# First head pair of an attention kernel: the second head's codes of k behind the second exponential, codes of q's second half one step later

## The chip, the cores and the metric

The kernel runs on one core of a Trainium2 chip. The metric is device time in microseconds (us), from launch to the end of the program. A profiled execution also has a span, from its first to its last instruction.

The core has five engines, each with its own queue that it works off in order, and they meet at semaphores: TensorE (PE in the profile; its weight loads are PEld), VectorE (DVE), ScalarE (ACT), GpSimd (POOL) and SyncE (SP), which here issues the DMAs.

## The reference

Attention with hashed masks over 4 batches of 8 heads (768 positions, 64 wide), followed by a mixture of 8 experts with one expert for each token. Cut to what matters:

```python
scale = 1.0 / np.sqrt(D)
q_bits = (np.einsum('bhsd,dk->bhsk', q, proj) > 0)          # 6 bits; k_bits alike
mask = q_bucket[:, :, :, None] == k_bucket[:, :, None, :]   # all 6 bits equal
scores = np.where(mask, scale * q @ k.T, -1e9)
attn = softmax(scores)
x = (attn @ v)                                              # 3072 tokens of 512
e = argmax(x @ w_gate, axis=1)
out = gate * (relu(x @ w1[e]) @ w2[e])
```

## The kernel before

**Tiling.** The 32 heads are worked in 16 pairs. A pair has six blocks of 128 queries for each of two heads, so 12 steps; there are 192 steps in all, and the list `steps` gives for each step i its pair, its group of three blocks, its block and its head. In pair 0 the first six steps are blocks 0, 1, 2 of head 0 and then blocks 0, 1, 2 of head 1; steps 6 to 11 take blocks 3, 4, 5, head 0 and head 1 in turn. After the attention the tokens, scattered by expert into a buffer in DRAM, are gathered and pass through the two products of each expert.

**A step.** `scores` (L220) makes 128 rows of scores with four products: q and k are each split into a high part (q1, k1) and a low part, and q2 and k2 carry the codes, 12 more rows that push a pair of unequal buckets far below all others. VectorE takes the maximum m (L228 to L230), `expo` (L233) lets ScalarE make p with its sums, `transposes` (L260) turns p on TensorE and ScalarE copies it out (L268), and `av` (L278) multiplies by v. The loop over i runs ahead: in round i it writes the scores of step i+2, then the exponential of step i+1, then the transposes of step i. Scores have two banks (`s`), transposes two (`t`), codes of q and some other small work one (`misc`).

**Operands.** For pairs from 1 on, q and k are split by GpSimd (`q_operands`, `k_operands`: L161 to L163 and L167 to L169), their codes are made by `pair_codes` (L143: a product into `misc` or `t` at L148, compared with 0 at L150, scaled at L151) and placed by DMA (`code_rows`, L176). The table `PREPARE` says in which round: for pair 1, both heads' q in round 2, codes and the first head's k in round 3.

Pair 0 has functions of its own. `first_k` (L181) makes one head's k1 and k2 and a product for its codes in both banks `t`; it returns a function that compares them (L200, VectorE, two instructions) and scales them (L201, ScalarE, two). `first_q` (L205) does the same for half of a head's q: a product into `misc` (L210), casts (L212, L213 on VectorE for the second half; L215, L216 on ScalarE for the first), the low part on GpSimd (L217), and a returned function that compares (L218, VectorE). The second halves are not needed before step 6 (head 0) and step 7 (head 1).

**What sets the order.** PE, DVE, ACT and SP carry out their work in the order in which the program writes it. GpSimd's work on q, k and codes is held in the order of writing too, each instruction by a dependence on the one before it:

```python
def in_turn(ins):
    ins = ins.ins
    if pinned:
        tc.add_manual_dep(ins, pinned.pop().name, mybir.DependencyInfo(mybir.DependencyClass.NoSync, mybir.DependencyReason.DATA),
                          reason="order of GpSimd's work on q, k and codes")
```

The pool of q's and k's raw tiles of pair 0 is closed (`start.close()`) in round 3.

Of the kernel before, what the change touches and what calls it, by code (L numbers as in the profile page):

```python
# [52 lines left out]
def bf(ap):  # L53
    return ap.bitcast(F32)
# [3 lines left out]
def lsh_attention_moe_kernel(ctx, tc, qkd, q2d, k2d, v, pjbd, wg, w1, w2, ident_in, tri_in, cols_in, eoff_in, ids_in, out):  # L58
# [64 lines left out]
# [5 lines that stand above are left out]
        if not in_turn_over:  # L128
            pinned.append(ins)
# [51 lines left out]
    def first_k(hh, low):  # L181
        kr = operands[0][0][hh][1]
        k1, k2 = operands[0][0][hh][4:6]
        cpss = []
        for x in range(2):
            cps = ps_t.tile([P, 512], F32, name="t")
            r0 = D + 32 * x
            PE.matmul(out=cps[r0:r0 + 32, 0:384], lhsT=pj, rhs=kr[:, 384 * x:384 * x + 384], start=True, stop=True)
            cpss.append(cps[r0:r0 + NCODE, 0:384])
        if hh:  # L190
            A.copy(out=k1, in_=kr)
        else:
            V.tensor_copy(out=k1, in_=kr)
        low.tensor_tensor(out=k2[0:D], in0=kr[0:D], in1=bf(k1[0:D]), op=ALU.subtract)

        def put_codes():
            for x in range(2):
                cs = slice(384 * x, 384 * x + 384)
                r0 = D + 32 * x
                V.tensor_scalar(out=k2[D:KM, cs], in0=cpss[x], scalar1=0.0, scalar2=cols[r0:r0 + NCODE, 2:3], op0=ALU.is_gt, op1=ALU.subtract)  # L200
                A.activation(k2[D:KM, cs], bf(k2[D:KM, cs]), AF.Copy, bias=0.0, scale=BIG)  # L201

        return put_codes

    def first_q(hh, c0):  # L205
        qr = operands[0][0][hh][0]
        q1, q2 = operands[0][0][hh][2:4]
        cps = ps_m.tile([P, 512], F32, name="misc")
        cs = slice(c0, c0 + 384)
        PE.matmul(out=cps[0:32, 0:384], lhsT=pj, rhs=qr[:, cs], start=True, stop=True)  # L210
        if c0:
            V.tensor_copy(out=q1[:, cs], in_=qr[:, cs])  # L212
            V.tensor_copy(out=q2[0:D, cs], in_=qr[0:D, cs])  # L213
        else:
            A.copy(out=q1[:, cs], in_=qr[:, cs])  # L215
            A.copy(out=q2[0:D, cs], in_=qr[0:D, cs])  # L216
        in_turn(G.tensor_tensor(out=q1[D:P, cs], in0=qr[D:P, cs], in1=bf(q1[D:P, cs]), op=ALU.subtract))  # L217
        return lambda: V.tensor_scalar(out=q2[D:KM, cs], in0=cps[0:NCODE, 0:384], scalar1=0.0, scalar2=cols[0:NCODE, 0:1], op0=ALU.is_gt, op1=ALU.subtract)  # L218
# [14 lines left out]
    def expo(s, m, sums, idx, moves):  # L233
        if moves:
            p = pdp.tile([P, S], F32, name="pd")
            to, of = p.rearrange("p (a c i) -> p c a i", a=4, i=SQ), s[:, 0:S].rearrange("p (c a i) -> p c a i", a=4, i=SQ)
        else:
            p = pp.tile([P, S], F32, name="p")
            to, of = p, s[:, 0:S]
        A.activation(to, of, AF.Exp, bias=m[:, 2:3], scale=m[:, 1:2], accum_out=sums[:, idx:idx + 1])  # L240
        return p

    def move(p, pt, hh):
        way = moved[next(writes) % 2]
        q = pdp.tile([P, 4, 6, SQ], F32, name="pq")
        to = way.rearrange("(a j) s k -> s j a k", a=4)

        def out():
            for x in range(4):
                SY.dma_start(out=to[x], in_=p[SQ * x:SQ * x + SQ].rearrange("j (a k) -> j a k", a=4))  # L250

        def back():
            SY.dma_start(out=q, in_=way.rearrange("p s (c i) -> p s c i", i=SQ))

        def turn():
            V.transpose(out=pt()[:, hh].rearrange("p c (s j) -> p c s j", j=SQ), in_=q.rearrange("p s c i -> p c s i"))

        return out, back, turn
# [305 lines left out]
    def sums_of(pr, g):  # L564
        if (pr, g) not in grp:
            grp[(pr, g)] = smp.tile([P, 6], F32, name="sums", bufs=4)
        return grp[(pr, g)]

    def run_expo(i):
        pr, g, jj, hh = steps[i]  # L570
        moves = i % 6 in MOVES.get((pr, g), ())
        p = expo(*soft.pop(i), sums_of(pr, g), 2 * jj + hh, moves)
        if moves:
            out, back, turn = move(p, partial(probs_t, pr, g, jj), hh)
            later.extend([(i, out), (i + 2, back)])
            turns.append((i + 5, turn))
        else:
            probs[i] = p

    def run_scores(i):  # L580
        pr, g, jj, hh = steps[i]
        soft[i] = scores(pr, 3 * g + jj, hh)
# [158 lines left out]
    first_codes = [first_k(0, V), first_q(0, 0)]  # L741
# [3 lines left out]
    run_scores(1)  # L745
    first_codes = [first_k(1, G), first_q(1, 0)]
    run_expo(0)
    for f in first_codes:
        f()
    SY.dma_start(out=h0[0][:, 384:S], in_=q2d[0][:, 384:S])  # L750
    prev, due, extra = None, [], {}
    for i, (pr, g, jj, hh) in enumerate(steps):
# [27 lines left out]
            prefill(i // 6 - 1)  # L780
        if i + 2 < len(steps):
            run_scores(i + 2)
        if 1 <= i < 3:
            first_q(i - 1, 384)()
        if i == 3:
            start.close()
        if i + 1 < len(steps):
            run_expo(i + 1)
        while late:
            late.pop(0)()  # L790
        sums = sums_of(pr, g)
# [439 lines left out]
```

## Time and profile before

| | us |
|---|---|
| median of 3 runs | 748.88 |
| the runs | 747.42, 748.88, 756.24 |
| profiled execution | 746.31 |
| its span | 744.5 |
| TensorE busy in the span | 717.5 (96%) |
| VectorE busy | 527.4 (71%) |
| ScalarE busy | 457.9 (62%) |
| GpSimd busy | 384.5 (52%) |

The profiled execution took 1.8 us more than its span. The mean granted TensorE clock was 0.993 of full speed. A row of the timeline reads: start in us, duration in us, engine, line, operation, output, input, shapes, count, and in brackets how long the engine had stood idle and what released it. Where several instructions of a kind follow each other they are merged into one row, with the time from the first start to the last end.

### The profile page before, as it was taken

How to read it: one execution, taken by the hardware profiler on the slowest of the kernel's cores; microseconds unless marked ns; L12 is line 12 of the kernel's file. 1: busy time of each engine (PE TensorE's matmuls, PEld its weight loads, DVE VectorE, ACT ScalarE, POOL GpSimd, SP SyncE). 2: the span in 40 equal slices, each digit the busy share in tenths (PEclk: the TensorE clock that was granted, in tenths of full speed). 3: DMA queues.
4: the chain of work that ended last, by engine and by line, in shares of the span. 5: the costliest groups of instructions: out<-in, count | busy, mean ns of one | idle time of the engine just before them, and what ended most of it. 6: DMA issues, size and time to landing. Idle time of an engine off the chain costs nothing.

```text
span 744.5 us, 16345 instructions
## 1 busy us (share of the span) xinstructions
PE 717.5 (96%) x5919; PEld 632.3 (85%) x5919; DVE 527.4 (71%) x1158; ACT 457.9 (62%) x941; POOL 384.5 (52%) x366
## 2 busy tenths in 40 slices
PE   6999999999999999999989998999999999999996
PEld 3788888877888778888777887999999999999994
DVE  6667776887887888887899776674747465566741
ACT  5888887777888678888677865343434334344430
POOL 2877337098436187634485242007474738364381
PEclk8999999999999999999999999999999999999999
DMA  5166666666666567666664531746556565657531
GB/s 185 50 192 165 195 182 189 187 194 189 178 183 190 170 203 196 166 181 188 176 180 131 160 90 59 209 105 177 146 175 152 189 165 161 188 154 226 165 91 43
DMA packets 85259, 121.45 MB, mean 163 GB/s; under 512 B 10758, under 2 KB 57382, under 8 KB 85168
## 3 DMA queue, kind: packets, MB, share of 16 engines
q1 hardware_dynamic: 80176, 107.61, 51.3%
q0 software_dynamic: 4992, 12.69, 4.9%
q8 instruction: 49, 0.80, 0.5%
q14 instruction: 42, 0.34, 0.1%
HBM read 79.04 MB, written 39.24 MB: 159 GB/s over the span
## 4 chain that ended last, share of the span: by engine, by line
PE 45%; issue 22%; POOL 13%; DVE 11%; DMA 5%; SPq 2%; ACT 1%; POOLq 0%; DVEq 0%
PE o L283 14%; POOL y L1007 10%; PE t L265 9%; PE s L225 9%; PE s L226 7%; DVE m L228 4%; DMA y<-yo,tags 2%; POOL yo L1005 1%; PE misc L315 1%; PE t L148 1%; DMA qk<-qkd 1%; DMA xr<-xs 1%; DVE m L230 1%; SPq L176 1%; ACT p L240 1%
## 5 line engine op out<-in xcount | busy, mean ns | idle before, releaser
L228 DVE TENSOR_REDUCE m<-s 128x1 f32<-128x768 f32 x192 | 182.6, 951 | 48.4 <-PE s L226 41.4
L240 ACT ACTIVATE p<-s,m 128x768 f32<-128x768 f32 x144 | 143.3, 995 | 42.0 <-DVE m L230 27.8
L225 PE MATMUL s<-k,q 128*128 128x512 f32 (+1 forms) x384 | 149.2, 389 | 7.8 <-ACT p L240 5.2
L283 PE MATMUL o<-pt,vt 128*64 128x128 f32 x2304 | 146.7, 277 | 0.2
L268 ACT COPY pt<-t 128x384 f32<-128x384 f32 x288 | 123.9, 482 | 34.3 <-PE t L265 31.2
L283 PEld LDWEIGHTS o<-pt,vt 128*64 128x64 f32 x2304 | 123.8, 137 | 14.8 <-issue 7.4
L226 PE MATMUL s<-k,q 76*128 76x512 f32 (+1 forms) x384 | 123.9, 343 | 0.2 <-DVE q L218 0.2
L265 PE MATMUL t<-ident,p 128*128 128x128 f32 x864 | 120.0, 274 | 3.2 <-DVE cr L150 3.1
L1007 POOL DMA_INDIRECT y<-yo,tags x89 | 103.3, 1161 | 25.2 <-issue 22.9
L225 PEld LDWEIGHTS s<-k,q 128*128 128x128 f32 x384 | 73.2, 191 | 44.4 <-issue 15.0
L265 PEld LDWEIGHTS t<-ident,p 128*128 128x128 f32 x864 | 99.0, 141 | 6.7 <-DVE cr L150 4.0
L965 ACT ACTIVATE hh<-hps 128x352 fp32r<-128x352 f32 (+3 forms) x56 | 28.0, 500 | 99.3 <-PE hps L979 88.6
L682 DVE TENSOR_TENSOR wlo<-wraw,whi 128x1024 fp32r<-128x1024 f32 x60 | 73.0, 1219 | 17.0 <-ACT whi L677 16.0
L226 PEld LDWEIGHTS s<-k,q 76*128 76x128 f32 x384 | 73.7, 192 | 9.3 <-ACT k L201 0.5
L998 PE MATMUL hps<-hh,wlo 128*128 128x436 f32 (+6 forms) x224 | 76.2, 340 | 0.0
L998 PE MATMUL hps<-hh,whi 128*128 128x448 f32 (+10 forms) x224 | 76.2, 340 | 0.0
L998 PE MATMUL hps<-hl,whi 128*128 128x436 f32 (+6 forms) x224 | 76.2, 340 | 0.0
L979 PE MATMUL hps<-xh,whi 128*128 128x352 f32 (+3 forms) x224 | 75.0, 335 | 0.0
L979 PE MATMUL hps<-xh,wlo 128*128 128x428 f32 (+6 forms) x224 | 74.8, 334 | 0.0
L979 PE MATMUL hps<-xl,whi 128*128 128x428 f32 (+6 forms) x224 | 74.8, 334 | 0.0
L1005 POOL TENSOR_TENSOR yo<-yt,tags 128x512 f32<-128x512 f32 (+3 forms) x25 | 23.4, 959 | 88.1 <-DVE yt L1000 88.0
L966 DVE SCALAR_TENSOR_TENSOR hl<-hps,hh 128x352 fp32r<-128x352 f32 (+3 forms) x56 | 31.7, 566 | 48.6 <-ACT hh L965 45.0
(225 smaller groups left out, 1202.1 us busy)
## 6 DMA issues: line engine op xcount, KB each, us to landing
wraw<-w SPq DMA_DIRECT2D x64, 512.0 KB
moved<-pd SPq DMA_DIRECT2D x192, 96.0 KB
pq<-moved SPq DMA_DIRECT2D x48, 384.0 KB
qk<-qkd SPq DMA_DIRECT2D x30, 384.0 KB
xs<-zrow SPq DMA_DIRECT2D x8, 910.0 KB
vt<-v SPq DMA_DIRECT2D x16, 384.0 KB
xr<-xs SPq DMA_DIRECT2D x12, 178.8 KB
xr<-xs SPq DMA_DIRECT2D x8, 227.5 KB
```

What stands on the lines that cost most here:

```text
L225: PE.matmul(out=s[:, c0:c1], lhsT=q1[:, qs], rhs=k1[:, c0:c1], start=True, stop=False)
L226: PE.matmul(out=s[:, c0:c1], lhsT=q2[0:KM, qs], rhs=k2[0:KM, c0:c1], start=False, stop=True)
L228: V.reduce_max(out=m[:, 0:1], in_=s[:, 0:S], axis=AX.X)
L240: A.activation(to, of, AF.Exp, bias=m[:, 2:3], scale=m[:, 1:2], accum_out=sums[:, idx:idx + 1])
L265: PE.transpose(out=t[:, i * P:i * P + P], in_=p[:, kc * P:kc * P + P], identity=ident)
L268: A.copy(out=dst, in_=src)
L283: PE.matmul(out=o[hh * D:hh * D + D, jj * P:jj * P + P], lhsT=vt[:, kc, hh * D:hh * D + D], rhs=pt[:, hh, kc], start=kc == 0, stop=kc == N ...
L682: loeng.tensor_tensor(out=lo[:, i:i + step], in0=cell["t"], in1=bf(hi[:, i:i + step]), op=ALU.subtract)
L966: V.scalar_tensor_tensor(out=hl, in0=hps[:, 0:C], scalar=0.0, in1=bf(hh), op0=ALU.max, op1=ALU.subtract)
L979: PE.matmul(out=hps[:, 0:w], lhsT=wt[:, c, fs], rhs=xt[:, c, 0:w], start=n == 0, stop=n == 3 * NDC - 1)
L998: PE.matmul(out=yps[:, 0:w], lhsT=wt[:, f, ds], rhs=ht[:, 0:w], start=n == 0, stop=n == 3 * NFC - 1)
L1007: rows_apart("out", G.indirect_dma_start(out=out_seg, out_offset=bass.IndirectOffsetOnAxis(ap=tags[:, i, 0:1].bitcast(I32), axis=0), in_=y ...
```

## The change

Two pieces of work in pair 0 are written later.

1. The returned functions of head 1's `first_k` and of the first half of its `first_q` were called right after the exponential of step 0. They are now called in round 0, behind the scores of step 2 and the exponential of step 1.
2. `first_q` for the second halves, with its returned function, was called in round 1 for head 0 and round 2 for head 1. It is now called in rounds 2 and 3. The pool is closed in round 4.

```diff
@@ -745,8 +745,6 @@
     run_scores(1)
     first_codes = [first_k(1, G), first_q(1, 0)]
     run_expo(0)
-    for f in first_codes:
-        f()
     SY.dma_start(out=h0[0][:, 384:S], in_=q2d[0][:, 384:S])
@@ -780,12 +778,15 @@
         if i + 2 < len(steps):
             run_scores(i + 2)
-        if 1 <= i < 3:
-            first_q(i - 1, 384)()
-        if i == 3:
+        if 2 <= i < 4:
+            first_q(i - 2, 384)()
+        if i == 4:
             start.close()
         if i + 1 < len(steps):
             run_expo(i + 1)
+        if i == 0:
+            for f in first_codes:
+                f()
```

The numbers of instructions stay the same on all engines. Three places in the queues show what moves. In the rows, q1_153 and q2_154 belong to head 0 of pair 0, q1_157, q2_158, k1_159 and k2_160 to head 1; other numbers name buffers and can differ between the two kernels.

ScalarE from the exponential of step 0 on, before:

```order
L240 ACTIVATE p_213,sums_212<-s_183,m_188 128x768
L201 ACTIVATE k2_160<-k2_160 12x384 x2
L240 ACTIVATE p_230,sums_212<-s_192,m_197 128x768
L268 COPY pt_232<-t_233 128x384
L268 COPY pt_232<-t_238 128x384
L240 ACTIVATE p_258,sums_212<-s_221,m_226 128x768
L268 COPY pt_260<-t_261 128x384
```

VectorE from the maximum of step 1 on, before:

```order
L228 TENSOR_REDUCE m_197<-s_192 128x1
L229 TENSOR_SCALAR m_197<-m_197 128x1
L230 TENSOR_SCALAR m_197<-m_197 128x1
L200 TENSOR_SCALAR k2_160<-t_201,cols_65 12x384
L200 TENSOR_SCALAR k2_160<-t_203,cols_65 12x384
L539 CAST tri_69<-lsb_147 128x128
L218 TENSOR_SCALAR q2_158<-misc_207,cols_65 12x384
L541 COPY run_72<-eoff_67 128x8
L228 TENSOR_REDUCE m_226<-s_221 128x1
```

ScalarE from the exponential of step 0 on, now:

```order
L240 ACTIVATE p_213,sums_212<-s_183,m_188 128x768
L240 ACTIVATE p_225,sums_212<-s_192,m_197 128x768
L201 ACTIVATE k2_160<-k2_160 12x384 x2
L268 COPY pt_232<-t_233 128x384
L268 COPY pt_232<-t_238 128x384
L240 ACTIVATE p_252,sums_212<-s_216,m_221 128x768
L268 COPY pt_254<-t_255 128x384
```

VectorE from the maximum of step 1 on, now:

```order
L228 TENSOR_REDUCE m_197<-s_192 128x1
L229 TENSOR_SCALAR m_197<-m_197 128x1
L230 TENSOR_SCALAR m_197<-m_197 128x1
L228 TENSOR_REDUCE m_221<-s_216 128x1
L539 CAST tri_69<-lsb_147 128x128
L541 COPY run_72<-eoff_67 128x8
L229 TENSOR_SCALAR m_221<-m_221 128x1
L230 TENSOR_SCALAR m_221<-m_221 128x1
L200 TENSOR_SCALAR k2_160<-t_201,cols_65 12x384
L200 TENSOR_SCALAR k2_160<-t_203,cols_65 12x384
L218 TENSOR_SCALAR q2_158<-misc_207,cols_65 12x384
```

The scaling of k2_160 stands behind the exponential of step 1 on ScalarE, and its comparison (L200) with that of q2_158 (L218) stands behind the maximum of step 2 (L228 to L230) on VectorE.

VectorE from the maximum of step 4 on, before:

```order
L228 TENSOR_REDUCE m_276<-s_271 128x1
L229 TENSOR_SCALAR m_276<-m_276 128x1
L230 TENSOR_SCALAR m_276<-m_276 128x1
L212 CAST q1_157<-qr_131 128x384
L213 CAST q2_158<-qr_131 64x384
L218 TENSOR_SCALAR q2_158<-misc_280,cols_65 12x384
L228 TENSOR_REDUCE m_318<-s_313 128x1
L229 TENSOR_SCALAR m_318<-m_318 128x1
L230 TENSOR_SCALAR m_318<-m_318 128x1
L150 TENSOR_SCALAR cr_340<-misc_335,cols_65 128x384
```

VectorE from the first cast behind the maximum of step 4 on, now:

```order
L212 CAST q1_153<-qr_129 128x384
L213 CAST q2_154<-qr_129 64x384
L218 TENSOR_SCALAR q2_154<-misc_274,cols_65 12x384
L228 TENSOR_REDUCE m_312<-s_307 128x1
L229 TENSOR_SCALAR m_312<-m_312 128x1
L230 TENSOR_SCALAR m_312<-m_312 128x1
L212 CAST q1_157<-qr_131 128x384
L213 CAST q2_158<-qr_131 64x384
L218 TENSOR_SCALAR q2_158<-misc_316,cols_65 12x384
L150 TENSOR_SCALAR cr_339<-misc_334,cols_65 128x384
```

Head 0's casts and codes (q1_153, q2_154) stand behind the maximum of step 4, where head 1's stood, and head 1's stand behind the maximum of step 5 and right ahead of the codes of pair 1 (L150).

GpSimd, from the low part of head 0's second half on (L217), then the work on q of pair 1 (L161 to L163), before:

```order
L217 TENSOR_TENSOR q1_153<-qr_129,q1_153 64x384
L217 TENSOR_TENSOR q1_157<-qr_131,q1_157 64x384
L161 CAST q1_299<-qk_142 64x768
L162 TENSOR_TENSOR q1_299<-qk_142,q1_299 64x768
L163 CAST q2_300<-qk_142 64x768
L161 CAST q1_303<-qk_144 64x768
L162 TENSOR_TENSOR q1_303<-qk_144,q1_303 64x768
L163 CAST q2_304<-qk_144 64x768
L167 CAST k1_301<-qk_142 64x768
```

GpSimd from the same instruction on, now:

```order
L217 TENSOR_TENSOR q1_153<-qr_129,q1_153 64x384
L161 CAST q1_293<-qk_142 64x768
L162 TENSOR_TENSOR q1_293<-qk_142,q1_293 64x768
L163 CAST q2_294<-qk_142 64x768
L161 CAST q1_297<-qk_144 64x768
L162 TENSOR_TENSOR q1_297<-qk_144,q1_297 64x768
L163 CAST q2_298<-qk_144 64x768
L217 TENSOR_TENSOR q1_157<-qr_131,q1_157 64x384
L167 CAST k1_295<-qk_142 64x768
```

Head 1's low part (q1_157) stands behind the six instructions on pair 1's q instead of ahead of them.

## The prediction

> **What bounds the kernel now.** I read the page first, then busy time by stages, then the chain of waits over the first 48 us, then the timelines of the five engines there. The page gives the execution that the sum is made against:
>
> ```profile
> span 744.5 us, 16345 instructions
> ```
>
> Busy time by stages (window, length, then busy time and count for TensorE, its weight loads, VectorE, ScalarE, GpSimd; granted clock, DMA share, GB/s):
>
> ```profile
> 0.00:26.00 26.00, 19.07 (x84) 10.83 (x85) 17.53 (x39) 16.26 (x33) 8.88 (x12) 0.87 0.40 132
> 26.00:30.00 4.00, 3.18 (x22) 2.52 (x21) 2.85 (x8) 4.00 (x10) 3.88 (x4) 1.00 0.07 14
> 30.00:100.00 70.00, 70.00 (x707) 59.96 (x706) 49.16 (x111) 57.90 (x129) 48.30 (x45) 1.00 0.60 176
> 100.00:500.00 400.00, 387.19 (x3769) 327.65 (x3768) 322.83 (x816) 291.16 (x639) 190.72 (x179) 1.00 0.58 168
> ```
>
> TensorE has holes and a granted clock of 0.87 before 26 us, lacks 0.82 us between 26 and 30, and from 30 to 100 us is busy for all 70.00 us. So a delay that reaches TensorE by 30 us has nothing to hide in for the next 70 us; between 100 and 500 us it idles 12.8 us in all, which a rival below uses. The change lies wholly before 30 us. The chain of waits there (start, us, what):
>
> ```profile
> 23.43 0.78 PE misc L148 x8
> ...
> 25.49 0.35 ACT pt L268
> ...
> 29.62 0.50 PE s L225
> ```
>
> Up to 25 us the chain runs over TensorE in its written order, then over ScalarE's exponentials and copies, and from 29.62 us (the scores of step 9) over TensorE again. Step 9's start is therefore the place where I take the balance: what it is late there, the end is late.
>
> **The change, first part: the second head's codes of k.** These rows are the present order; s is a block of scores, m its maximum and scale, p its exponentials:
>
> ```profile
> 11.09 0.21 DVE L230 TENSOR_SCALAR m<-m 128x1 f32<-128x1 f32 x1
> ...
> 11.33 1.27 DVE L200 TENSOR_SCALAR k<-t,cols 12x384 fp32r<-12x384 f32 x2
> ...
> 11.93 0.29 PE L226 MATMUL s<-k,q 76*128 76x256 f32 x1
> 11.98 1.18 ACT L201 ACTIVATE k<-k 12x384 fp32r<-12x384 f32 x2 [0.80 <-DVE k L200]
> ...
> 13.19 0.99 ACT L240 ACTIVATE p<-s,m 128x768 f32<-128x768 f32 x1
> ...
> 14.41 0.77 PE L225 MATMUL s<-k,q 128*128 128x512 f32 x1 [1.20 <-ACT p L240]
> ...
> 14.79 0.21 DVE L230 TENSOR_SCALAR m<-m 128x1 f32<-128x1 f32 x1
> ...
> 15.10 0.99 ACT L240 ACTIVATE p<-s,m 128x768 f32<-128x768 f32 x1
> ```
>
> m of step 1 is ready at 11.09 + 0.21 = 11.30, but ScalarE first scales the codes (11.98 to 13.16) and starts exponential 1 at 13.19. Put first, it starts at about 11.35: 1.8 us earlier. Scores 3, which waited for its bank, now wait longer for the codes. VectorE's work from 11.33 to 14.79 + 0.21 = 15.00 is the same set in both orders, 3.67 us, but it must now begin with the maximum of step 2, whose scores end at 11.93 + 0.29 = 12.22. Started at 12.27 it ends at 15.94, with the two code instructions (1.27) and the codes of q last: k's codes are out at about 15.3, not 12.6. ScalarE's scaling ends at 15.9 instead of 13.16, and exponential 2 follows it after the two copies of step 0 (15.10 - 13.19 - 1.08 for the exponential with its accumulator = 0.83): 16.8 against 15.10, 1.7 late. TensorE's second three transposes of step 0 write the bank that the later code instruction reads, so they start at 15.4; the scores of step 3 begin at 16.0 against 14.41, 1.6 late.
>
> This loss is nearly made good by the second part, since the code product of q's second half no longer stands behind those scores:
>
> ```profile
> 15.96 1.49 PE L210 MATMUL misc<-qr,pj 128*32 128x384 f32 x2
> 17.38 1.54 PE L265 MATMUL t<-ident,p 128*128 128x128 f32 x6
> 18.58 0.78 PE L225 MATMUL s<-k,q 128*128 128x512 f32 x1
> ...
> 21.81 0.48 PE L225 MATMUL s<-k,q 128*128 128x512 f32 x1
> ...
> 22.61 0.82 PE L265 MATMUL t<-ident,p 128*128 128x128 f32 x6
> ...
> 23.36 0.85 PE L148 MATMUL misc<-qk,pj 128*32 128x384 f32 x8
> ...
> 24.14 0.50 PE L225 MATMUL s<-k,q 128*128 128x512 f32 x1
> ...
> 25.55 0.47 PE L225 MATMUL s<-k,q 128*128 128x512 f32 x1
> ```
>
> From 15.96 to 17.38 it held TensorE for 1.42 us. So the transposes of step 1 start at 16.0 + 1.55 (scores to next start, 15.96 - 14.41) = 17.55, scores 4 at 18.75 against 18.58, and its maximum 0.18 late. The first of the moved products now lies at 20.3, where the second lay (20.13), so scores 5 begin about when they did, 21.8. Sum of the first part: 0 to 0.2 us late. The moved product, two casts and code instruction of each head are the same number as before; no DMA moves past another, and the pool that is closed one step later frees nothing that is used here.
>
> **Second part: what stands behind q's second half.** VectorE makes the casts of head 0 (q1_153) where it made those of head 1 (q1_157), right behind the maximum of step 4:
>
> ```profile
> 20.13 1.11 PE L210 MATMUL misc<-qr,pj 128*32 128x384 f32 x2
> ...
> 21.55 0.35 DVE L212 CAST q<-qr 128x384 fp32r<-128x384 f32 x1
> ...
> 22.84 0.96 DVE L228 TENSOR_REDUCE m<-s 128x1 f32<-128x768 f32 x1
> ...
> 24.02 0.21 DVE L230 TENSOR_SCALAR m<-m 128x1 f32<-128x1 f32 x1
> ```
>
> Head 0's first cast is thus at 21.55 + 0.18 = 21.73. The maximum of step 5 follows at 23.02 (22.84 + 0.18); 24.02 + 0.21 - 22.84 = 1.39 us later its m is ready, at 24.41; then come head 1's casts and codes, 22.84 - 21.55 = 1.29 us, to 25.7. Only then can the codes of pair 1 (L148), which write the one bank that the codes of q use, begin: 25.7 against 23.36, 2.3 late. They stand ahead of scores 6 on TensorE: these start at 26.45 against 24.14, and the transposes of step 4 end near 28.1.
>
> On GpSimd it is worse, because its queue is kept in the order in which the program writes q, k and code work:
>
> ```profile
> 21.98 1.05 POOL L217 TENSOR_TENSOR q<-qr,q 64x384 fp32r<-64x384 f32 x1 [3.13 <-DVE q L212]
> ...
> 23.10 0.82 POOL L161 CAST q<-qk 64x768 fp32r<-64x768 f32 x1
> ...
> 29.42 0.82 POOL L163 CAST q<-qk 64x768 fp32r<-64x768 f32 x1
> ...
> 30.28 0.83 POOL L167 CAST k<-qk 64x768 fp32r<-64x768 f32 x1
> ...
> 36.52 0.83 POOL L169 CAST k<-qk 64x768 fp32r<-64x768 f32 x1
> ...
> 37.04 0.50 PE L225 MATMUL s<-k,q 128*128 128x512 f32 x1
> ```
>
> Before, both subtractions of L217 came ahead of pair 1's q, six instructions from 23.10 to 30.28, 7.18 us. Now head 0's takes the place of head 1's (21.98 + 0.18 = 22.16), the six follow from 23.28 to 30.46, and only then comes head 1's, 1.05 us long: 31.51. Scores 7 read it and start at 31.57 against 25.55: **6.0 us late**. Behind scores 7 wait, on TensorE, everything; ScalarE and VectorE run dry after step 6. TensorE idles from 28.1 to 31.57. GpSimd itself ends only 1.2 us late, pair 1's k at 36.52 + 0.83 + 1.2 = 38.6, and scores 12, which read it and began at 37.04, come some 7 us later: covered.
>
> **From step 7 to step 9.** At full clock a step costs scores 0.80 (21.81 to 22.61) plus transposes 0.75 (22.61 to 23.36) = 1.55; scores 9 need exponential 7, that is scores 0.98, the maximum with m 1.43, an exponential 1.0 and gaps: 3.48 after 31.57, 35.05, so 5.4 late. At half clock a step costs 1.55 (14.41 to 15.96) plus 1.20 (17.38 to 18.58) = 2.75, two of them 5.5: 37.07, so 7.45 late. The trace shows when the clock is halved (stages of 3.4 us, cut where the granted clock changes):
>
> ```profile
> 10.50:13.90 3.40, 1.87 (x10) 1.30 (x10) 3.17 (x9) 2.44 (x5) 0.95 (x1) 1.00 0.68 231
> 13.90:17.30 3.40, 2.89 (x6) 1.34 (x6) 2.19 (x6) 2.20 (x6) 0.00 (x0) 0.50 0.00 0
> 17.30:20.70 3.40, 3.40 (x12) 2.52 (x12) 1.76 (x5) 1.94 (x4) 1.04 (x1) 0.50 0.00 0
> 20.70:24.10 3.40, 3.40 (x26) 2.09 (x24) 3.20 (x9) 2.34 (x6) 1.97 (x3) 1.00 0.00 0
> ```
>
> After 3.4 us with 1.87 us of work the clock fell to 0.50; after 3.4 us with 2.89 it stayed there; after a full 3.40 it rose. With the same stages carried on (24.1, 27.5, 30.9), the stage from 27.5 holds 0.6 us of work, the next 2.8, the third is full: half clock to 37.7, and the 0.6 us of it after step 9's start cost 0.6 x 1.20/2.75 = 0.3 more: 7.7. With other cuts the half clock lasts from 3.4 to 6.8 us after 31.57; 3.4 gives 1.24 slow steps and 0.76 fast ones, 36.2, 6.5 late; 6.8 gives 7.45 and 1.3 x 0.44, 8.0. I take 7.5, toward the cut of this trace.
>
> The Trainium skill, page "TensorE: Matmul & The Clock Gate", section "Part 1: The HAM clock gate", says that the window is free-running, 3413 ns long, that one idle window halves the clock, and that one busy window of sustained work restores it. The length agrees with the trace (half clock from 13.9 to 20.7, 6.8 us, twice that), but the trace halved the clock after a window 55% busy and kept it halved after one 85% busy. If a window must be wholly idle, a pause of 3.5 us would hardly ever hold one, and the loss would be 5.4: that is rival 1.
>
> **Sum.** First part 0.2, GpSimd's queue +5.8 more at scores 7, back to +5.4 at step 9 at full clock because steps 5 and 6 are ready by then, and +2.1 for half clock: +7.5 us, slower by 1.0%. The profiled execution took 746.3, under all three runs shown (747.4 to 756.2, median 748.9). I add to the midpoint of 746.3 and 748.9, 747.6: 755.1.
>
> **The rivals.**
> 1. The clock stays full through the pause, as it would if only a stage without any work halved it. Then 747.6 + 5.4 = 753.0. For it: a pause of 3.5 us is short. Against: the fall at 13.9 us came with pauses of 1.2 us each. Chance 0.17.
> 2. Not slower: TensorE's later waits swallow the delay. From 100 to 500 us it idles 12.8 us; if those waits end at times that GpSimd and the DMA queues set for themselves, 7.5 us of delay vanish there and the time is 747.6. It decides at 7.5 of the 12.8 us being such waits. Against it, who waited for whom (us in total, times, the longest), on GpSimd from 30 to 300 us and on TensorE from 26 to 400:
>
> ```profile
> POOL q L161 <- PE s L225: 52.9, 5, 12.2
> ...
> PE s L225 <- POOL q L162: 1.4, 2, 0.9
> ```
>
> GpSimd stood 52.9 us in five waits (the longest 12.2) until TensorE's scores freed a buffer, so it follows TensorE and brings the delay along; TensorE waited 1.4 us for it. Chance 0.12.
> 3. Slower by over 2%, 15.0 us: half clock would have to last. Beyond the 5.4, a microsecond of it costs 1.20/2.75 = 0.44 us, so 9.6 us more need 22 us of half clock; time 762.6 or more. Steps that wait on ScalarE could keep TensorE at 85%, which did not suffice at 13.9. Against: from step 7 on two steps stand ready. Chance 0.03.
>
> **How the numbers follow.** My forecast, about 7.5 us slower, has 0.67; its own range is 746.3 + 6.5 = 752.8 to 748.9 + 8.0 = 756.9. A clear gain over 2% would need 15 us where the part touched is 20 us long: 0.01, and it is the remaining case. The 8-in-10 range takes in rival 1 on the lower base with the 1.4 us given back that TensorE later waits for GpSimd's q (746.3 + 5.4 - 1.4 = 750.3), and above one more stage of 3.4 us at half clock, at 0.44 a microsecond (748.9 + 8.0 + 1.5 = 758.4). About 2% is what a measurement of this kernel can tell from no change; the forecast and rivals 1 and 2 lie within it: 0.96; faster 0.01, slower 0.03.
>
> **What would show it.** Right: exponential 1 near 11.4, scores 3 near 16.0, scores 5 within 0.3 of 21.8, L148 near 25.7, head 1's second L217 behind six instructions near 30.5, scores 7 just after it, a granted clock of 0.5 for some microseconds from 31, scores 9 between 36 and 37.5, and from there the same distances as before. Wrong: scores 7 before 28 us; TensorE's idle time between 100 and 500 us smaller by several microseconds; or a loss that grows after step 12.

## The result and the profile after

| | before | changed |
|---|---|---|
| median of 22 runs each, us | 750.5 | 756.5 |
| lowest, highest, us | 745.79, 759.21 | 752.49, 765.54 |
| ratio to before, 95% interval | | 1.0078, 1.0053 to 1.0103 |
| span of the profiled execution, us | 744.5 | 750.7 |

The change makes the kernel 0.78% slower (0.53 to 1.03%), some 5.9 us of 750.5; that is less than the 2% that the prediction took as the least that can be told from no change, and yet clear of zero. Executions over 1.5% longer than the fastest of their kernel, which show a lower granted clock (0.974 to 0.980 in four of the changed kernel's 22, 0.985 to 0.996 in the others), are left out of the ratios but not of the medians, and where a profile is one of them (first and sixth experiment) its span isn't used. The profiled spans differ by 6.2 us. The page of the changed kernel (TensorE, VectorE, ScalarE and GpSimd have the same numbers of instructions as before):

```profile
span 750.7 us, 16346 instructions
```

Its busy time by stages (columns as in the prediction):

```profile
0.00:26.00 26.00, 17.75 (x64) 10.04 (x64) 16.30 (x35) 15.57 (x30) 7.60 (x10) 0.93 0.39 132
30.00:100.00 70.00, 69.68 (x668) 60.18 (x668) 48.40 (x109) 57.27 (x126) 43.25 (x40) 0.97 0.56 161
100.00:500.00 400.00, 387.54 (x3802) 327.24 (x3799) 323.63 (x820) 293.60 (x649) 197.08 (x184) 1.00 0.58 169
```

Against before, TensorE has done less work in the first 26 us (64 instructions against 84, 17.75 us of busy time against 19.07). From 30 to 100 us it is busy for 69.68 of 70 us, from 100 to 500 us it idles 12.46 us against 12.81. So the loss arises before 40 us, and nearly all of it stays: 6.6 us at the start of scores 9, 6.2 at the end of the span.

The first part of the change in the timeline of the changed kernel:

```profile
11.86 0.99 ACT L240 ACTIVATE p<-s,m 128x768 f32<-128x768 f32 x1 [0.21 <-PE t L188]
...
14.88 1.27 DVE L200 TENSOR_SCALAR k<-t,cols 12x384 fp32r<-12x384 f32 x2
15.52 1.18 ACT L201 ACTIVATE k<-k 12x384 fp32r<-12x384 f32 x2 [2.58 <-DVE k L200]
...
16.57 0.69 PE L225 MATMUL s<-k,q 128*128 128x512 f32 x1
...
21.81 0.48 PE L225 MATMUL s<-k,q 128*128 128x512 f32 x1
...
22.26 1.04 POOL L217 TENSOR_TENSOR q<-qr,q 64x384 fp32r<-64x384 f32 x1 [10.82 <-DVE q L212]
```

Exponential 1 starts at 11.86, the comparisons of k's codes (L200) at 14.88, and scores 3 at 16.57, against 13.19, 11.33 and 14.41 before. Yet scores 5 start at 21.81, at the same time as before; what that says of the first part is taken up in the first experiment. Head 0's low part (L217) starts at 22.26, where before head 1's did at 21.98.

Then VectorE, GpSimd and TensorE:

```profile
24.27 1.80 POOL L162 TENSOR_TENSOR q<-qk,q 64x768 fp32r<-64x768 f32 x1
...
24.43 1.87 DVE L212 CAST q<-qr 128x384 fp32r<-128x384 f32 x1
...
26.12 0.85 POOL L163 CAST q<-qk 64x768 fp32r<-64x768 f32 x1
26.21 0.97 DVE L213 CAST q<-qr 64x384 fp32r<-64x384 f32 x1
...
26.92 0.95 POOL L161 CAST q<-qk 64x768 fp32r<-64x768 f32 x1
...
27.21 0.61 DVE L218 TENSOR_SCALAR q<-misc,cols 12x384 fp32r<-12x384 f32 x1
27.88 1.51 PE L148 MATMUL misc<-qk,pj 128*32 128x384 f32 x8 [3.10 <-DVE q L218]
...
29.32 0.80 PE L225 MATMUL s<-k,q 128*128 128x512 f32 x1
...
30.70 0.99 POOL L217 TENSOR_TENSOR q<-qr,q 64x384 fp32r<-64x384 f32 x1
...
31.90 0.78 PE L225 MATMUL s<-k,q 128*128 128x512 f32 x1
...
34.30 0.50 PE L225 MATMUL s<-k,q 128*128 128x512 f32 x1
...
36.26 0.50 PE L225 MATMUL s<-k,q 128*128 128x512 f32 x1 [0.32 <-ACT p L240]
```

Two things stand out. Head 1's casts L212 and L213 on VectorE take 1.87 and 0.97 us; the same two took 0.35 and 0.34 before, and head 0's first one takes 0.35 here. The first begins at 24.43, while GpSimd's subtraction L162 runs (24.27 to 26.07), and is done 0.2 us after it; the second begins at 26.21 beside L163 (26.12 to 26.97) and is done 0.2 us after that. L148 has waited 3.10 us for the codes behind them, scores 6 start at 29.32, not 24.14. And GpSimd's L217 for head 1 stands behind six instructions, as forecast, done at 31.69; scores 7 start at 31.90, but no wait is noted: TensorE only came there then. So in this execution the queue that the prediction named is hidden, by 0.2 us, under casts that it had not priced.

TensorE's clock (stages cut where it changes):

```profile
23.48:26.90 3.42, 1.29 (x8) 0.64 (x6) 3.35 (x5) 1.97 (x6) 3.29 (x3) 1.00 0.00 0
26.90:30.30 3.40, 2.42 (x10) 1.03 (x11) 1.51 (x3) 0.00 (x0) 3.27 (x4) 0.50 0.02 5
30.30:33.70 3.40, 3.40 (x15) 3.17 (x14) 1.39 (x4) 1.90 (x4) 3.24 (x4) 0.50 0.00 0
33.70:37.10 3.40, 3.08 (x21) 2.47 (x20) 2.58 (x6) 3.28 (x9) 3.26 (x4) 0.99 0.07 16
```

Half clock from 26.9 to 33.7 us, hence 1.51 us for L148 (0.85 before) and 0.80 for a first product of scores (0.50).

### The profile page after: what moved, and what is told of

Read it like the earlier page. It is cut to its first block, busy times and chain, and to the rows that moved or that the text cites. A ratio compares the mean times of both kernels' runs of the same rounds, so it can differ in the third digit from the quotient of the medians.

```text
span 750.7 us, 16346 instructions
## 1 busy us (share of the span) xinstructions
PE 722.1 (96%) x5919; PEld 636.7 (85%) x5919; DVE 529.4 (71%) x1158; ACT 458.2 (61%) x941; POOL 387.1 (52%) x366
## 4 chain that ended last, share of the span: by engine, by line
PE 45%; issue 21%; POOL 13%; DVE 12%; DMA 6%; SPq 2%; ACT 1%; POOLq 0%; another core or an unknown queue 0%; DVEq 0%; ACTq 0%
PE o L283 15%; POOL y L1008 11%; PE s L225 10%; PE t L265 9%; PE s L226 8%; DVE m L228 4%; DMA y<-yo,tags 2%; DMA qk<-qkd 2%; PE misc L315 2%; POOL yo L1006 1%; PE t L148 1%; DVE m L230 1%; DMA xr<-xs 1%; SPq L250 1%; ACT pd L240 1%
## 5 line engine op out<-in xcount | busy, mean ns | idle before, releaser
L228 DVE TENSOR_REDUCE m<-s 128x1 f32<-128x768 f32 x192 | 182.6, 951 | 52.2 <-PE s L226 49.4
L225 PE MATMUL s<-k,q 128*128 128x512 f32 (+1 forms) x384 | 151.5, 395 | 4.7 <-ACT p L240 3.0
L226 PE MATMUL s<-k,q 76*128 76x512 f32 (+1 forms) x384 | 126.2, 349 | 0.0
L1008 POOL DMA_INDIRECT y<-yo,tags x89 | 105.6, 1187 | 25.2 <-issue 22.6
L161 POOL CAST q<-qk 64x768 fp32r<-64x768 f32 x30 | 24.8, 828 | 84.6 <-PE s L225 68.3
```

Source lines behind the costliest of these rows:

```text
L225: PE.matmul(out=s[:, c0:c1], lhsT=q1[:, qs], rhs=k1[:, c0:c1], start=True, stop=False)
L226: PE.matmul(out=s[:, c0:c1], lhsT=q2[0:KM, qs], rhs=k2[0:KM, c0:c1], start=False, stop=True)
L228: V.reduce_max(out=m[:, 0:1], in_=s[:, 0:S], axis=AX.X)
L1008: rows_apart("out", G.indirect_dma_start(out=out_seg, out_offset=bass.IndirectOffsetOnAxis(ap=tags[:, i, 0:1].bitcast(I32), axis=0), in_=y ...
```

## The experiments

The start of a step in absolute time moves by about 2 us between executions of the same kernel, with the clock of the first 20 us (the ninth run below). The distance from the start of scores 5 to the start of scores 9, called D here, moves far less: it is 7.81 and 7.79 us in the two profiles of before, and 14.45 and 14.78 in those of the changed kernel. The table uses it. It has two limits. It doesn't see what is lost ahead of scores 5. And wherever q's second halves are written later, it holds head 1's code product, which before lay ahead of scores 5: 1.1 us with its wait. Ratios are to runs of before on the same chip; before's median was 745.0 us in the set of the first four runs and 736.9 in that of the next four, so times and spans of different sets are not compared, and the expectations' spans hold for the first set alone.

| run | casts of head 1, us | scores 7 wait for GpSimd, us | D, us | ratio, 95% interval |
|---|---|---|---|---|
| before | 0.35, 0.34 | no | 7.81 | 1 |
| changed | 1.87, 0.97 | no | 14.45 | 1.0078 (1.0053 to 1.0103) |
| changed, second profile | 1.87, 0.97 | 0.77 | 14.78 | |
| codes of k alone | 0.35, 0.34 | no | 7.88 | 1.0022 (0.9991 to 1.0052) |
| q's second halves alone | 1.87, 0.97 | 0.88 | 14.83 | 1.0110 (1.0063 to 1.0156) |
| pair 1's q behind head 1's low part | 0.35, 0.34 | no | 10.18 | 1.0047 (1.0018 to 1.0076) |
| head 1's casts on ScalarE | on ScalarE | 3.98 | 14.93 | 1.0142 (1.0069 to 1.0215) |
| head 1's low part on VectorE | 1.87, 0.97 | no | 12.33 | 1.0077 (1.0037 to 1.0117) |
| products in TensorE's pause | 1.87, 0.97 | 1.47 | 13.69 | 1.0095 (1.0045 to 1.0144) |
| a bank of their own for q's codes | 0.35, 0.35 | no | 9.16 | 1.0014 (0.9977 to 1.0051) |
| ScalarE's scaling alone | 0.35, 0.35 | no | 7.80 | 0.9995 (0.9959 to 1.0032) |

**The two parts apart.** The first run has only the first part:

```diff
     run_expo(0)
-    for f in first_codes:
-        f()
...
             run_expo(i + 1)
+        if i == 0:
+            for f in first_codes:
+                f()
```

> Before with the first part alone: the second head's codes of k are called in round 0, q's second halves stay in rounds 1 and 2. Reading: start of the scores of step 9 (before 29.6, changed 36.3) and the span (744.5, 750.7). If VectorE's casts are slow only beside GpSimd's work on pair 1's q: head 1's casts take 0.35 and 0.34, and what is left is the late codes, scores 3 near 16.0, scores 9 at 30.2 to 31.2, span 745 to 746. If the late codes of k were the cause of the whole loss: scores 9 near 36, span near 750.

D is 7.88 and scores 9 start at 29.45 (29.62 before). The casts take 0.35 and 0.34. So the first part by itself makes none of the loss behind scores 5. Ahead of them, where D is blind, scores 3 at 15.89 are 1.5 us late, as expected. That scores 5, at 21.57, are not late against the 21.81 of before shows little, because TensorE's clock was halved for 3.4 us in this profile (14.95 to 18.36) and for 6.8 in that of before. Over all twelve profiles scores 5 start between 19.31 and 21.81 in the four without the first part, and between 20.13 and 22.24 in the eight with it. The ratio, 1.0022, is 1.6 us, from -0.7 to 3.9. Whether the late codes cost 1 or 2 us ahead of scores 5 stays open.

The second run has only the second part:

```diff
-        if 1 <= i < 3:
-            first_q(i - 1, 384)()
-        if i == 3:
+        if 2 <= i < 4:
+            first_q(i - 2, 384)()
+        if i == 4:
```

> Before with the second part alone: q's second halves one round later, the codes of k as before. If the loss is VectorE's casts beside GpSimd's subtraction: head 1's two casts take 2 to 3 us together instead of 0.7, scores 6 start past 27, scores 9 at 34 to 36, span 749 to 751. If it is GpSimd's queue: the casts may take 0.7, but scores 7 start within 0.1 us after the end of head 1's low part (L217), TensorE having waited for it. If part one were needed for the loss: scores 9 below 31.

TensorE from L148 on:

```profile
25.38 0.85 PE L148 MATMUL misc<-qk,pj 128*32 128x384 f32 x8 [3.10 <-DVE q L218]
...
29.25 0.79 PE L225 MATMUL s<-k,q 128*128 128x512 f32 x1 [0.88 <-POOL q L217]
...
34.14 0.48 PE L225 MATMUL s<-k,q 128*128 128x512 f32 x1
```

Both causes show: casts of 1.87 and 0.97 ahead of L148 (scores 6 start at 26.16; the expectation had said past 27), and scores 7 released by GpSimd's L217 after a wait of 0.88. D is 14.83, as in the changed kernel: the whole growth of D comes from the second part alone.

**Both causes away.** GpSimd's work on pair 1's q is written one round later, so that it stands behind head 1's low part:

```diff
-        {(0, 2): [(q_operands, (0,)), (q_operands, (1,))], (0, 3): [(pair_codes, ()), (k_operands, (0,))],
+        {(0, 3): [(q_operands, (0,)), (q_operands, (1,)), (pair_codes, ()), (k_operands, (0,))],
```

> Changed kernel, but GpSimd's six instructions on pair 1's q are written one round later, behind head 1's low part. Neither GpSimd's queue nor an overlap of the casts with its work is left. If these two are the loss: casts 0.35 and 0.34, L148 near 25.7, scores 6 near 26.5, scores 7 near 28, scores 9 at 31 to 32.5, span 746 to 747.5. If the late codes of k or the place of L148 behind the casts make the loss by themselves: scores 9 at 34 or later, span 749 or more.

```profile
25.07 0.85 PE L148 MATMUL misc<-qk,pj 128*32 128x384 f32 x8 [0.96 <-DVE q L218]
...
31.33 0.50 PE L225 MATMUL s<-k,q 128*128 128x512 f32 x1
```

The casts are back at 0.35 and 0.34, L148 waits 0.96 instead of 3.10, scores 9 start at 31.33. Nothing changed on TensorE, VectorE or ScalarE but the waiting: of the 6.6 us by which D had grown, 4.3 are gone (14.45 to 10.18).

**The queue alone.** Head 1's two casts go to ScalarE, GpSimd's order stays as changed:

```diff
-        if c0:
+        if c0 and not hh:
             V.tensor_copy(out=q1[:, cs], in_=qr[:, cs])
```

> Changed kernel, but head 1's two casts of the second half are made by ScalarE (0.51 us each, as its casts of the first half). GpSimd's queue stays. If both matter and each hides the other: L148 near 25.3, scores 6 near 26, then TensorE waits until L217 is done near 31.6, scores 9 at 35 to 37.3, span 749.9 to 752. If only the slow casts matter: scores 7 before 29, scores 9 at 31 to 32.5, span 746 to 747.5.

```profile
25.64 0.85 PE L148 MATMUL misc<-qk,pj 128*32 128x384 f32 x8 [0.43 <-DVE q L218]
...
32.03 0.80 PE L225 MATMUL s<-k,q 128*128 128x512 f32 x1 [3.98 <-POOL q L217]
...
37.17 0.70 PE L225 MATMUL s<-k,q 128*128 128x512 f32 x1
```

L148 comes at 25.64, and then TensorE waits 3.98 us for L217. D is 14.93: with the slow casts gone, the queue makes the whole growth of D by itself, at the size that the prediction had given it (5.4 at full clock, 7.45 with half clock; here 7.1, with the clock at half from about 31). The ratio rests on six executions of this kernel, and its interval reaches past 2%.

**The casts alone.** Head 1's low part is made by VectorE, behind its codes, so that scores 7 don't hang on GpSimd:

```diff
-        in_turn(G.tensor_tensor(out=q1[D:P, cs], ...))
+        if not (c0 and hh):
+            in_turn(G.tensor_tensor(out=q1[D:P, cs], ...))
...
+            if c0 and hh:
+                V.tensor_tensor(out=q1[D:P, cs], in0=qr[D:P, cs], in1=bf(q1[D:P, cs]), op=ALU.subtract)
```

> Changed kernel, but head 1's low part of the second half is made by VectorE, behind its codes, so scores 7 no longer hang on GpSimd's queue; the casts still lie beside GpSimd's subtraction. If slow casts and queue each hide the other: casts again 1.9 and 1.0, scores 6 near 29, scores 7 near 32, scores 9 near 36, span 749.5 to 751.5. If the queue alone makes the loss: scores 7 before 29, scores 9 below 33, span 746 to 748.

TensorE (lines after 217 are 7 higher in this kernel):

```profile
27.16 0.85 PE L148 MATMUL misc<-qk,pj 128*32 128x384 f32 x8 [3.10 <-DVE q L221]
...
29.34 0.48 PE L232 MATMUL s<-k,q 128*128 128x512 f32 x1
...
33.42 0.50 PE L232 MATMUL s<-k,q 128*128 128x512 f32 x1
```

L148 again waits 3.10 us for the codes, and scores 7 start right behind the transposes, without a wait. D is 12.33, not the 14.5 that the theory of two causes hiding each other had called for. It is 4.5 us above before and 2.2 above the run with neither cause (10.18): that much the slow casts add. The remaining 2.1 us, to 14.45, belong to the queue and the half clock together, since in this execution the clock also stayed full, which the expectation had missed. The ratio, 1.0077, is the same as the changed kernel's; its interval is too wide to tell 4.5 from 6.6 us.

**The clock.** Four products are added in TensorE's pause ahead of L148. They write a bank that nobody reads:

```diff
+        if i == 3:
+            o = ps_o.tile([P, 512], F32, name="o")
+            for _ in range(4):
+                PE.matmul(out=o[:, 0:384], lhsT=ident, rhs=operands[1][0][0][0][:, 0:384], start=True, stop=True)
```

> Changed kernel with four products of 128x384 in fp32 added ahead of L148, into a bank that nobody reads: TensorE works (about 2.6 us) while it would wait for head 1's codes. If the half clock has its share in the loss: granted clock 1.0 at 27 to 34, L148 0.85 instead of 1.51, scores 9 at 34.8 to 35.6, span 749 to 750. If the clock costs nothing: scores 9 near 36.3, span 750.7; if the added work itself delays: later than 36.3.

```profile
24.40 2.75 PE L857 MATMUL o<-qk,ident 128*128 128x384 f32 x8
27.67 0.85 PE L148 MATMUL misc<-qk,pj 128*32 128x384 f32 x8 [0.53 <-DVE q L218]
...
31.57 0.50 PE L225 MATMUL s<-k,q 128*128 128x512 f32 x1 [1.47 <-POOL q L217]
...
35.28 0.50 PE L225 MATMUL s<-k,q 128*128 128x512 f32 x1 [0.70 <-ACT p L240]
```

The clock stays full, L148 takes 0.85, and scores 9 start at 35.28, in the range expected. But now TensorE reaches scores 7 early and waits 1.47 us for L217. D is 13.69 against 14.45 and 14.78: full clock is worth about 1 us here, since the queue takes the rest of it. And it is 1.4 above the 12.33 of the run before, which also had full clock and the slow casts but no queue: that is what the queue adds on top of the casts. The ratio, 1.0095, doesn't show a gain of 1 us.

**What is left without both causes.** On top of the third run, the code products of q's second halves use another bank, so that L148 doesn't wait for head 1's codes:

```diff
-        cps = ps_m.tile([P, 512], F32, name="misc")
+        cps = ps_o.tile([P, 512], F32, name="o") if c0 else ps_m.tile([P, 512], F32, name="misc")
```

> As the run with pair 1's q behind head 1's low part (scores 9 at 31.3, span 746.0), and the code products of q's second halves use the bank of the attention output, idle until step 7, so that L148 doesn't wait for head 1's codes. If that wait is what was left of the loss: L148 near 24.5, scores 6 near 25.2, scores 9 at 29.6 to 30.7, span 744.5 to 745.5. If the late codes of k are: scores 9 at 31 or later, span 746.

```profile
24.33 0.85 PE L148 MATMUL misc<-qk,pj 128*32 128x384 f32 x8
...
30.59 0.50 PE L225 MATMUL s<-k,q 128*128 128x512 f32 x1
```

L148 doesn't wait any more, scores 9 start at 30.59, as expected, and D is 9.16 against 10.18: the wait for the bank was 1.0 us. Of the last 1.35 us of D, 1.1 are head 1's code product, which before lay ahead of scores 5 and now lies behind them (it waits 0.39 us and holds TensorE some 0.75); that is work moved across the mark, not lost by itself. The ratio is 1.0014 (0.9977 to 1.0051).

**ScalarE's scaling alone**, on the kernel before: VectorE's comparisons stay, only the two scalings of the second head's codes go behind exponential 1.

```diff
                 V.tensor_scalar(out=k2[D:KM, cs], in0=cpss[x], ...)
-                A.activation(k2[D:KM, cs], bf(k2[D:KM, cs]), AF.Copy, bias=0.0, scale=BIG)
+                if not hh:
+                    A.activation(k2[D:KM, cs], bf(k2[D:KM, cs]), AF.Copy, bias=0.0, scale=BIG)
...
             run_expo(i + 1)
+        if i == 0:
+            ...
+                A.activation(k2[D:KM, cs], bf(k2[D:KM, cs]), AF.Copy, bias=0.0, scale=BIG)
```

> Kernel before, but only ScalarE's two scalings of the second head's codes of k are put behind exponential 1; VectorE's comparisons and q's second halves stay. If the scaling in front was what scores 3 waited for: scores 3 about 0.7 earlier against the maximum of step 2, and scores 9 at 28.9 to 29.6. If the chain over ScalarE from 25 us on sets step 9: scores 9 at 29.4 to 29.8, no gain. Either way within 0.2% of before, span 743.5 to 745.

The first two products of scores 3 (lines 1 higher in this kernel):

```profile
12.63 0.47 PE L226 MATMUL s<-k,q 128*128 128x512 f32 x1
14.57 0.47 PE L227 MATMUL s<-k,q 76*128 76x512 f32 x1 [1.47 <-DVE q L219]
```

The first one starts right behind the transposes of step 0 (its bank is free early), but the second waits 1.47 us for VectorE's codes of q. The wait only changed its place. D is 7.80 and the ratio 0.9995: no gain. Scores 9 at 27.64 lie below both ranges expected, but they are no gain either, as the next run shows.

**Both kernels once more.**

> The kernel before, unchanged, profiled once more: how far the start of the scores of step 9 (29.6 in the first profile) moves from one execution to the next with the windows of the clock. If those windows don't matter: 29.4 to 29.8. If they do: between 27.6 (all of 12 to 22 us at full clock) and 31.

> The changed kernel, unchanged, profiled once more: scores 7 held by GpSimd's queue or not. Head 1's casts again 1.9 and 1.0 and scores 6 near 28 to 29.5 in any case. If TensorE's clock is halved while it waits: scores 7 at 31.5 to 32.3, scores 9 near 36.3. If it stays full: scores 7 waits for L217 and starts near 31.5, scores 9 near 35.2.

The kernel before had scores 9 at 27.46 this time, just below the range expected and 2.2 us earlier than in its first profile, because its clock stayed full through steps 3 and 4; scores 5 were just as much earlier (19.67 against 21.81). The changed kernel:

```profile
26.99 0.50 PE L225 MATMUL s<-k,q 128*128 128x512 f32 x1
...
30.08 0.79 PE L225 MATMUL s<-k,q 128*128 128x512 f32 x1 [0.77 <-POOL q L217]
...
34.91 0.47 PE L225 MATMUL s<-k,q 128*128 128x512 f32 x1
```

Scores 6 start at 26.99, a microsecond ahead of the range expected, the transposes behind them end near 29.3, and scores 7 wait 0.77 us for L217. Here the queue decided, as forecast; in the first profile it was 0.2 us short of deciding. With the clock halved from 27.8 to 34.6 us scores 9 start at 34.91 (the range expected without the half clock; scores 5 had come 1.7 us earlier than in the first profile). The two spans of this pair are 742.6 and 751.2.

## Why the prediction was right, and which step was not

**Direction and size.** Forecast were +7.5 us, with 6.5 to 8.0 from the first edge to the last, and 755.1 us; measured are a ratio that makes 5.9 us (4.0 to 7.7), and 756.5. The size was set 1.6 us too high, and the base 2.9 us too low: before's median over 22 runs is 750.5, not the 747.6 that the sum was added to. That 756.5 came within 1.4 us of the forecast is in part luck, since the two errors are of opposite sign.

**First part, 0 to 0.2 us late at scores 5.** Not decided. The single steps were right to 0.6 us (exponential 1 at 11.86, scores 3 at 16.57), and scores 5 start at 21.81 in both profiles; but that mark moves by 2 us from one execution to the next, and D begins only there.

**L148 at 25.7, 2.3 late.** Wrong in size: 27.88, 4.5 late. The step that failed is "then come head 1's casts and codes, 22.84 - 21.55 = 1.29 us". Its rows came from an execution in which GpSimd wasn't working beside these casts; behind the changed order it is, and they took 2.84 us, with codes and gaps 3.4 instead of 1.29 us. The order showed the six instructions in that place, and the sum had even dated them (23.28 to 30.46); that they run beside the casts was not priced. That the neighbour is the cause is shown by the two runs that write GpSimd's work on pair 1's q behind head 1's low part: there the casts stand in the same place and take 0.35 and 0.34 or 0.35 again.

The Trainium skill, page "SBUF — State Buffer", section "Who interferes with whom", has the rule: VectorE's copies and casts can use a second pair of ports that it shares with GpSimd, and whichever of the two issues first keeps the pair for its whole instruction while the other blocks. The traces agree: in every run in which the casts stand beside GpSimd's L162 and L163 they take 1.87 and 0.97 us and end 0.2 us after GpSimd's instruction.

**GpSimd's queue, L217 from 30.46 to 31.51, scores 7 at 31.57.** Right to 0.4 us in the first profile (30.70 to 31.69, 31.90), and the queue alone gives the whole growth of D (fourth run, 14.93). But it wasn't the only thing that held scores 7: the slow casts brought TensorE there at the same time. The two causes overlap. Taking the casts away leaves D at 14.93, taking the queue away leaves 12.33, taking both leaves 10.18. An account with only one of them would still have fitted the time; only the runs that take each away separate them.

**Half clock, from 30.9 to 37.7.** Right in kind and length (6.8 us), wrong in place: 26.9 to 33.7. TensorE ran dry at 24.8, not at 28.1, since L148 was later than forecast, so part of the half clock fell into its pause and less into the work behind. That is why scores 9 came at 36.26 rather than 37.07, and the loss at 6.6 rather than 7.5 there. In the fourth run, where the queue alone stops TensorE, the half clock lasted from 30.8 to 37.65: kind and cause as forecast, the place by the luck of the cut.

**From step 9 on nothing given back.** Right but for 0.4 us: scores 12 start at 43.69 against 37.04, 6.65 us late, the span is 6.2 us longer, 0.4 less than the 6.64 at scores 9, and TensorE's idle time from 100 to 500 us is 0.35 us smaller. Rival 2 is out. Rival 1, a clock that stays full, didn't hold for the changed kernel in either profile.

**What stays open.** Whether a pause halves the clock. The stages of the run with head 1's low part on VectorE, cut on the grid of its earlier changes of clock:

```profile
22.29:25.70 3.41, 1.64 (x8) 0.77 (x8) 3.31 (x6) 2.44 (x6) 3.22 (x4) 1.00 0.00 0
25.70:29.10 3.40, 1.94 (x16) 1.23 (x17) 2.62 (x5) 0.00 (x0) 3.32 (x3) 1.00 0.02 5
```

These held 1.64 and 1.94 us of TensorE's work, and the clock stayed at 1.00. In the kernel before a stage with 1.87 halved it. So busy time doesn't decide alone. The Trainium skill's rule that one idle window halves the clock (page "TensorE: Matmul & The Clock Gate", section "Part 1: The HAM clock gate") fits the first case, in which no stage was idle, but not the second, as busy time is counted here. What is counted instead, no run here tells. Open too is what the first part costs ahead of scores 5.

## What to carry to other kernels

When a step is moved later in a program whose queues are kept in order of writing, list on each engine what it now stands behind, the engine nobody was thinking of too: here six GpSimd instructions of the next pair's work, 7.2 us long, got in front of one that the next scores needed. Then list what will run at the same time: a duration from the old trace holds only beside the old neighbours, and one of VectorE's casts took over five times its own beside GpSimd's work. Where a stall has two causes that end within a fraction of a microsecond of each other, removing one understates it: here, of the 4.3 us of D that went with both, taking away the casts alone gave back nothing and taking away the queue alone 2.1, with a clock that stayed full besides. Make the run without both, and then put each back.

## What the runs showed of the hardware

VectorE's casts from SBUF to SBUF wait for GpSimd: 128x384 in 1.87 us instead of 0.35 beside a GpSimd subtraction, 64x384 in 0.97 instead of 0.34 beside a GpSimd cast. VectorE's work that reads PSUM doesn't: L218 took 0.61 us in the rows above while GpSimd's L161 ran, as before. It goes the other way too. In the run with head 1's low part on VectorE, its subtraction started first:

```profile
27.14 0.56 DVE L223 TENSOR_TENSOR q<-qr,q 64x384 fp32r<-64x384 f32 x1
```

and GpSimd's own subtraction, which began beside it, took 2.15 us where 1.80 to 1.84 is usual:

```profile
27.23 2.15 POOL L162 TENSOR_TENSOR q<-qk,q 64x768 fp32r<-64x768 f32 x1
```

The clock's state at the start of the program isn't the same in every execution: scores 0 took 0.49 us for their first product in the first profile of before and 0.79 to 0.80 in ten of the other eleven profiles, although the column of the granted clock reads 1.00 there (it shows no change before 13 us in any profile). With the place at which the stages of the clock are cut (in before at 13.9 and 20.7, in the changed kernel at 16.7 and 20.1), it moves the first 20 us by about 2 us, a third of the effect studied here. A distance between two marks behind that stretch, D, was the same to 0.1 us in the two profiles of before and to 0.4 us in those of the changed kernel.
